# Q's second projection moved up behind kv, one mixer chunk moved ahead of the outputs, and x's blocks fetched in 4 loads

## The chip, the cores and the metric

The kernel runs on one NeuronCore of a Trainium2 chip. The metric is device time in microseconds of one execution. TensorE (PE in the profile; PEld is its weight loads), VectorE (DVE), ScalarE (ACT), GpSimd (POOL) and SyncE (SP, which issues the DMA loads and stores) run their own instruction streams in order and wait for each other on semaphores.

## The reference

Per batch (8 of them, 576 tokens) there is a linear attention over 8 heads with 128 exponential features, and then a token mixer of rank 32 and a two-layer network of width 2048:

```python
def phi(x):
    proj = np.einsum('bhsd,df->bhsf', x, w_phi)
    proj = proj - np.max(np.abs(proj), axis=-1, keepdims=True)
    return np.concatenate([np.exp(proj), np.exp(-proj)], axis=-1)
q_p, k_p = (phi(q), phi(k))
kv = np.einsum('bhsf,bhsd->bhfd', k_p, v)
z = np.sum(k_p, axis=2)
num = np.einsum('bhsf,bhfd->bhsd', q_p, kv)
den = np.einsum('bhsf,bhf->bhs', q_p, z)[..., None] + 1e-06
x = num / den                     # heads side by side: (8, 576, 512)
u = x + (x.transpose(0, 2, 1) @ U @ V).transpose(0, 2, 1)
out = u + np.maximum(u @ w_ch1, 0.0) @ w_ch2
```

## The kernel before

**Attention** goes by pairs of heads, four pairs to a batch, 32 in all. A pair (`Pair`, named b_j) has seven steps on TensorE: `s_project_k0` (products pkt, pk00, pk01), `s_out` of the pair before it (xpt, xp0, xp1), `s_project_k1` (pk10, pk11, pqt), `transposes` of the pair after it, `s_project_q0` (pq0), `s_kv` (kv_ps) and `s_project_q1` (pq1). Each q projection runs through a chain: ScalarE copies it (L394), GpSimd takes a maximum over partitions (L395), VectorE subtracts it (L396), ScalarE takes two exponentials (L397, L398); `s_out` needs the result, and it uses q1's (qp1) last, in xp1.

From batch 2 on (`SPLIT`), q and k come in as blocks (`raw`, 4 loads of 64 KB each for k and for q), which VectorE turns in place (L347) and splits into two parts, `T0` for k and `T1` for q (L350 on ScalarE, L351 on VectorE). `T1` has one buffer, so the next pair's T1 waits until pq1 has been computed, and the loads for the pair after that wait until T1 has been made from the block buffer. VectorE's L347 for a later pair stands ahead of L396 of qp1 in VectorE's order.

**The mixer** of batch g is cut into 32 chunks (`Mixer.chunks`): `hidden(f)` (product ph, 12 matrix products, then h_hi on ScalarE and h_lo on VectorE, L666) and `add(f)` (o, 12 products), f from 0 to 15, in the order h0, h1, a0, h2, a1, ... h15, a14, a15. ph has one PSUM bank, so a hidden chunk waits for the h_lo of the one before. `Pace.step()` puts the chunks of the batch before between the attention steps, 28 per batch; 4 are held back (`HELD`) until the batch's end.

**The end of a batch** is `tokens()`: the token mixing down (pp) and up (vp), x with the mixing added is stored to DRAM (`u_dram`, L618), and read back as blocks (`y`, L646, 16 loads), which VectorE turns (L652) and splits with ScalarE into uT_hi and uT_lo, from which the next mixer starts. The residual rows `st` are read from `u_dram` too (L690) and added at the end (L700). Attention products and vp share three PSUM banks (tag "at") in turn.

The order on TensorE is the written one from the tenth pair on; on the other engines, and on SyncE's queue, a scheduler places the instructions ahead of the run. Three chunks' worth of mixer weights are read again in each batch (`stream`, L218).

Of the kernel before, what the change touches and what calls it, by code (L numbers as in the profile page):

```python
# [21 lines left out]
P = 128  # L22
# [3 lines left out]
def tile_kernel(  # L26
# [12 lines left out]
    nc = tc.nc  # L39
    B, H, S, D = q.shape  # L40
# [91 lines left out]
    def scratch(name, dt=F32, shape=(2, 512)):  # L132
        return moe.tile([P, *shape], dt, tag="wide", bufs=NW, name=name)
# [132 lines left out]
    class Pair:  # L266
# [276 lines left out]
        def s_kv(self):  # L543
            self.kv_tail()
            self.kv_main(0, self.kp0)
            self.kv_main(1, self.kp1)
            self.kv_done()

        def s_out(self, x, xt):
            self.out_tail(xt)  # L550
# [70 lines left out]
    class Mixer:  # L621
        def __init__(self, g, x):
            self.g, self.x = g, x
            self.uT_hi = moe.tile([P, NCC, 512], F32R, tag="uT_hi", name=f"uT_hi{g}")
            self.uT_lo = moe.tile([P, NCC, 512], F32R, tag="uT_lo", name=f"uT_lo{g}")
            self.o, self.h = None, {}

        def transposes(self, t):
            pt = ps(f"pt{self.g}_{t}", "at" if 0 < self.g and t < 2 or self.g >= B - 1 else "o")
# [10 lines left out]

        def load_blocks(self):
            self.y = home.tile([P, NCC, SM], F32, tag="w_late", name=f"y{self.g}")
            for c in range(NCC):
                for i in range(4):
                    cs = slice(c * P + i * Q, c * P + (i + 1) * Q)
                    nc.sync.dma_start(  # L646
                        out=self.y[i * Q:(i + 1) * Q, c, :].rearrange("r (j e) -> r j e", e=Q),
                        in_=u_dram[self.g][:, cs].rearrange("(j r) e -> r j e", r=Q))

        def turn_blocks(self, c):  # L650
            y = self.y[:, c, :]
# [3 lines left out]
        def hidden(self, f):  # L655
            ph = ps(f"ph{self.g}_{f}", "at" if self.g >= B - 1 and f % 2 == 0 else "ph")
            n = 0
            for c in range(NCC):
                for l, r in ((0, self.uT_hi), (0, self.uT_lo), (1, self.uT_hi)):
                    mm(  # L660
                        ph, w1_part(f, l, c), r[:, c, :], start=(n == 0), stop=(n == 3 * NCC - 1))
                    n += 1
            h_hi = moe.tile([P, 512], F32R, tag="h_hi", bufs=2, name=f"h_hi{self.g}_{f}")
            h_lo = moe.tile([P, 512], F32R, tag="h_lo", bufs=2, name=f"h_lo{self.g}_{f}")
            on_act = nc.scalar.activation(out=h_hi, in_=ph, func=AF.Relu)  # L665
            on_dve = nc.vector.scalar_tensor_tensor(  # L666
                out=h_lo, in0=ph, scalar=0.0, in1=f32(h_hi), op0=ALU.max, op1=ALU.subtract)
            self.h[f] = (h_hi, h_lo)
            if self.g == 0:
                made.append((on_act, on_dve))  # L670
            if f in STREAM:
                stream(0, self.g, f)

        def add(self, f):
            if self.o is None:
                self.o = [ps(f"o{self.g}_{t}", "o") for t in range(4)]
            h_hi, h_lo = self.h.pop(f)
            for t in range(4):
                cs = slice(t * P, (t + 1) * P)
                for n, (l, r) in enumerate(((h_hi, 0), (h_hi, 1), (h_lo, 0))):  # L680
                    mm(
                        self.o[t], l[:, cs], w2_t[f][:, r, :],
                        start=(f == 0 and n == 0), stop=(f == NFC - 1 and n == 2))
            if f in STREAM:
                stream(1, self.g, f)
            if f == NFC - 3 and self.g < B:
                self.res = []
                for t in range(0, 4, 2):
                    st = scratch(f"st{self.g}_{t}")
                    nc.sync.dma_start(out=st, in_=u_rows(self.g)[:, t:t + 2, :])  # L690
                    self.res += [st[:, 0, :], st[:, 1, :]]
            if f == NFC - 1:
                self.finish()

        def finish(self):
            g = self.g
            for t in range(4):
                if g < B:
                    st = self.res[t]
# [101 lines left out]
    def tokens(tk, fill):  # L801
# [11 lines left out]
        other()  # L813
        pace.step()
        tk.down(1)
        other()
        pace.step()
        tk.up(0)
        tk.up(1)
        if tk.b >= SPLIT:  # L820
            tk.up(2)
            tk.up(3)
            m = Mixer(tk.b, tk.x)
            m.load_blocks()
            pace.step()
            other()
            pace.step()
            tk.up(NT)
            mix(len(todo) - HELD)
            for c in range(NCC):  # L830
                m.turn_blocks(c)
                mix(c % 2)
            todo.extend(m.chunks())
            return
# [36 lines left out]
    if True:  # L871
# [18 lines left out]
        for n, (b, j) in enumerate(pairs):  # L890
# [8 lines left out]
                    weights(LOADS[n])  # L899
            if nxt is not None:  # L900
                step(nxt.s_project_k0)
            step(cur.s_out, x, xt)
            if nxt is not None:
                step(nxt.s_project_k1)
# [4 lines left out]
            if j == NPAIR - 1:  # L909
                fill = []  # L910
                if nxt is not None:
                    fill = [far.transposes, nxt.s_project_q0, nxt.s_kv, nxt.s_project_q1]
                if b == 0:
                    pieces.extend(first_tokens(tk))
                    pieces.pop(0)()
# [11 lines left out]
            else:  # L927
# [7 lines left out]
                        pace.step()  # L935
                step(nxt.s_project_q0)
                step(nxt.s_kv)
                step(nxt.s_project_q1)
            cur, nxt = nxt, far
        mix(len(todo) - HELD)  # L940
        x = moe.tile([P, NT, C], F32, tag="x", name="x_tail")
# [39 lines left out]
```

## Time and profile before

| | |
|---|---|
| median of three executions | 1217.95 us (1217.53 to 1222.39) |
| the profiled execution's own time | 1218.95 us |
| its span, first to last instruction | 1217.2 us |
| TensorE busy | 1143.4 us (94%) |
| VectorE busy | 678.6 us (56%) |
| ScalarE busy | 536.9 us (44%) |
| GpSimd busy | 204.0 us (17%) |
| DMA bytes moved | 110.29 MB, mean 91 GB/s |

Read it as one long stream of matrix products with small gaps: the gaps, and stretches in which the granted clock is low, are all that can be won without taking products away. Batches 0 and 1 run until about 240 us, the paired stretches of batches 2 to 7 with a mixer beside them until about 1010 us, and the rest is mixer alone.

### The profile page before, as it was taken

The numbers are of one execution on the slowest core, as the hardware profiler recorded it, in microseconds if no ns is written. First come the engines' busy times: TensorE is split into PE (matmuls) and PEld (weight loads), VectorE is DVE, ScalarE is ACT, GpSimd is POOL, SyncE is SP. The second block draws the span as 40 slices with busy tenths as digits, with TensorE's granted clock in tenths as the row PEclk, the third lists the DMA queues.
The fourth block names the chain that finished last, engine by engine and source line by source line (L and its number), as shares of the span: only waits on it lengthen the run. The fifth ranks groups of instructions, "written<-read, shape, count | busy, mean of one in ns | idle before, by whom it ended". The sixth has DMA issues, their size and how long they took to land.

```text
span 1217.2 us, 22306 instructions
## 1 busy us (share of the span) xinstructions
PE 1143.4 (94%) x8845; PEld 940.3 (77%) x8845; DVE 678.6 (56%) x1482; ACT 536.9 (44%) x1151; POOL 204.0 (17%) x154
## 2 busy tenths in 40 slices
PE   8989988999998999899998999899999999999998
PEld 6767866778887887677787887687877878888886
DVE  5567798765556656754556566765656533312111
ACT  6678877454434544343434544344434431011110
POOL 4234453211110121011110121011201110000000
PEclk8999999999999999998999999999999999999999
DMA  5785421422353234422353233422342115410201
GB/s 144 224 264 199 134 57 20 138 65 65 82 117 94 52 63 112 102 49 63 82 118 93 55 64 106 106 66 55 92 102 80 36 53 160 121 52 15 75 15 35
DMA packets 247944, 110.29 MB, mean 91 GB/s; under 512 B 212640, under 2 KB 225184, under 8 KB 247840
## 3 DMA queue, kind: packets, MB, share of 16 engines
q1 hardware_dynamic: 247520, 108.34, 33.4%
q8 instruction: 70, 1.15, 0.4%
q10 hardware_dynamic: 320, 0.52, 0.1%
q14 instruction: 34, 0.28, 0.1%
HBM read 86.80 MB, written 22.02 MB: 89 GB/s over the span
## 4 chain that ended last, share of the span: by engine, by line
PE 65%; DVE 14%; SPq 6%; ACT 6%; DMA 5%; issue 2%; POOL 1%; DVEq 0%; POOLq 0%; ACTq 0%
PE o L79 24%; PE ph L79 23%; PE kv_ps L79 6%; PE xp L79 4%; SPq L291 3%; SPq L646 3%; DMA raw<-in_q_dram 3%; PE pq L79 2%; DVE T L351 2%; PE pk L79 2%; PE pp L79 1%; DVE uT_lo L259 1%; DVE h_lo L666 1%; DVE x L615 1%; DMA raw<-in_k_dram 1%
## 5 line engine op out<-in xcount | busy, mean ns | idle before, releaser
L79 PE MATMUL ph<-uT_hi,w 128*128 128x512 f32 x1152 | 387.9, 398 | 12.3 <-DVE h_lo L666 11.0
L79 PE MATMUL o<-w,h_hi 128*128 128x512 f32 x1152 | 358.8, 397 | 0.8 <-ACT h_hi L665 0.7
L79 PEld LDWEIGHTS ph<-uT_hi,w 128*128 128x128 f32 x1152 | 217.9, 189 | 63.3 <-DVE h_lo L666 14.7
L79 PEld LDWEIGHTS o<-w,h_hi 128*128 128x128 f32 x1152 | 213.9, 190 | 46.6 <-ACT h_hi L665 2.1
L79 PE MATMUL ph<-uT_lo,w 128*128 128x512 f32 x576 | 226.7, 394 | 2.4 <-DVE uT_lo L259 2.4
L79 PE MATMUL o<-w,h_lo 128*128 128x512 f32 x576 | 222.2, 394 | 0.3 <-DVE h_lo L666 0.3
L666 DVE SCALAR_TENSOR_TENSOR h_lo<-ph,h_hi 128x512 fp32r<-128x512 f32 x144 | 98.5, 684 | 220.0 <-ACT h_hi L665 219.7
L665 ACT ACTIVATE h_hi<-ph 128x512 fp32r<-128x512 f32 x144 | 85.7, 595 | 296.5 <-PE ph L79 296.2
L395 POOL PARTITION_ALL_REDUCE qp<-qp x64 | 128.8, 2012 | 339.5 <-ACT qp L394 339.2
L79 PEld LDWEIGHTS o<-w,h_lo 128*128 128x128 f32 x576 | 109.0, 190 | 24.2 <-DVE h_lo L666 0.8
L79 PEld LDWEIGHTS ph<-uT_lo,w 128*128 128x128 f32 x576 | 109.2, 190 | 23.6 <-DVE uT_lo L259 2.9
L79 PE MATMUL xp<-kv,qp 128*64 128x65 f32 x2048 | 87.5, 241 | 42.3 <-ACT qp L397 17.2
L79 PEld LDWEIGHTS xp<-kv,qp 128*64 128x64 f32 x2048 | 76.1, 153 | 55.3 <-ACT qp L397 21.9
L351 DVE TENSOR_TENSOR T<-raw,T 64x512 fp32r<-64x512 f32 x96 | 68.5, 714 | 34.7 <-ACT T L350 32.0
L395 POOL PARTITION_ALL_REDUCE qp_t<-qp_t x32 | 25.6, 800 | 358.9 <-ACT qp_t L394 358.9
L397 ACT ACTIVATE qp<-qp 128x512 f32<-128x512 f32 x64 | 40.2, 629 | 93.4 <-DVE qp L396 93.3
L350 ACT CAST T<-raw 64x512 fp32r<-64x512 f32 x96 | 59.4, 619 | 38.1 <-PE pq L79 36.8
L79 PE MATMUL kv_ps<-vb,kp 128*64 128x65 f32 x2048 | 70.0, 224 | 0.0
L79 PEld LDWEIGHTS kv_ps<-vb,kp 128*64 128x64 f32 x2048 | 63.8, 137 | 6.9 <-issue 2.0
L385 ACT ACTIVATE kp<-kp 128x512 f32<-128x512 f32 x64 | 40.3, 630 | 63.3 <-DVE kp L382 63.3
L347 DVE STREAM_TRANSPOSE raw<-raw 128x512 f32<-128x512 f32 x48 | 34.1, 711 | 47.2 <-DMA raw<-in_k_dram 27.7
L155 POOL INT64_ADD w_ab<-w_ab x32 | 43.6, 1363 | 71.7 <-DVE w_ab L151 59.8
(119 smaller groups left out, 1282.2 us busy)
## 6 DMA issues: line engine op xcount, KB each, us to landing
w<-kept SPq DMA_DIRECT2D x46, 512.0 KB, 3.8
words<-in_moe_w_ch_dram SPq DMA_DIRECT2D x32, 512.0 KB, 7.4
vb<-in_v_dram SPq DMA_DIRECT2D x64, 128.0 KB, 3.0
u_dram<-x SPq DMA_DIRECT2D x32, 256.0 KB, 2.1
st<-u_dram SPq DMA_DIRECT2D x16, 512.0 KB, 3.9
out_dram<-st SPq DMA_DIRECT2D x32, 256.0 KB, 2.1
y<-u_dram SPq DMA_DIRECT2D x112, 64.0 KB, 2.4
raw<-in_k_dram SPq DMA_DIRECT2D x96, 64.0 KB, 2.3
```

Of the source, the lines that this page charges most:

```text
L79: ins = nc.tensor.matmul(*args, **kw)
L155: nc.gpsimd.int64_add(a64, a64, b64)
L291: self.loaded = nc.sync.dma_start(out=to[i * Q:(i + 1) * Q], in_=src[b, self.h0 + i // 2, 0:SM, cs].rearrange("(j c) r -> c j r", c=Q))
L347: nc.vector.transpose(out=x_, in_=x_)
L350: nc.scalar.copy(out=m[here, s, :], in_=x_[here])
L351: nc.vector.tensor_sub(m[there, s, :], x_[here], f32(m[here, s, :]))
L385: nc.scalar.activation(out=kp[:, :, 0:F], in_=kp[:, :, F:2 * F], func=AF.Exp)
L395: nc.gpsimd.partition_all_reduce(qp[:, 0, :], qp[:, 1, :], P, ReduceOp.absmax)
L397: nc.scalar.activation(out=qp[:, 0, :], in_=qp[:, 1, :], func=AF.Exp)
L646: nc.sync.dma_start(out=self.y[i * Q:(i + 1) * Q, c, :].rearrange("r (j e) -> r j e", e=Q), in_=u_dram[self.g][:, cs].rearrange("(j r) e - ...
L665: on_act = nc.scalar.activation(out=h_hi, in_=ph, func=AF.Relu)
L666: on_dve = nc.vector.scalar_tensor_tensor(out=h_lo, in0=ph, scalar=0.0, in1=f32(h_hi), op0=ALU.max, op1=ALU.subtract)
```

## The change

Seven edits. (1) From batch 2 on, `s_project_q1` is issued inside `s_kv`, right behind the kv products, and the chunk that stood after it now stands as a second one between `s_project_k0` and the previous pair's `s_out`. (2) At the end of such a batch the fill list is one shorter, and the token products come in twos, with a chunk between. (3) `y` is fetched by 4 loads of 256 KB instead of 16 of 64 KB, each for 32 partitions and all four groups of columns. (4) The residual loads are issued after the second `down`, in a method of their own. (5) The streamed weights' loads are issued two chunks (`hidden`) or one (`add`) later in the code. (6) `tk.late` replaces an equal condition. (7) Line numbers behind the edits move by 2 to 10.

```diff
@@ -545,6 +545,8 @@
             self.kv_main(0, self.kp0)
             self.kv_main(1, self.kp1)
             self.kv_done()
+            if self.split:
+                self.s_project_q1()
 
         def s_out(self, x, xt):
             self.out_tail(xt)
@@ -623,7 +625,7 @@
             self.g, self.x = g, x
             self.uT_hi = moe.tile([P, NCC, 512], F32R, tag="uT_hi", name=f"uT_hi{g}")
             self.uT_lo = moe.tile([P, NCC, 512], F32R, tag="uT_lo", name=f"uT_lo{g}")
-            self.o, self.h = None, {}
+            self.o, self.h, self.res = None, {}, None
 
         def transposes(self, t):
             pt = ps(f"pt{self.g}_{t}", "at" if 0 < self.g and t < 2 or self.g >= B - 1 else "o")
@@ -640,12 +642,11 @@
 
         def load_blocks(self):
             self.y = home.tile([P, NCC, SM], F32, tag="w_late", name=f"y{self.g}")
-            for c in range(NCC):
-                for i in range(4):
-                    cs = slice(c * P + i * Q, c * P + (i + 1) * Q)
-                    nc.sync.dma_start(
-                        out=self.y[i * Q:(i + 1) * Q, c, :].rearrange("r (j e) -> r j e", e=Q),
-                        in_=u_dram[self.g][:, cs].rearrange("(j r) e -> r j e", r=Q))
+            of = u_dram[self.g].rearrange("(j r) (c i e) -> i r c j e", r=Q, i=4, e=Q)
+            for i in range(4):
+                nc.sync.dma_start(
+                    out=self.y[i * Q:(i + 1) * Q].rearrange("r c (j e) -> r c j e", e=Q),
+                    in_=of[i])
 
         def turn_blocks(self, c):
             y = self.y[:, c, :]
@@ -668,8 +669,8 @@
             self.h[f] = (h_hi, h_lo)
             if self.g == 0:
                 made.append((on_act, on_dve))
-            if f in STREAM:
-                stream(0, self.g, f)
+            if f - 2 in STREAM:
+                stream(0, self.g, f - 2)
 
         def add(self, f):
             if self.o is None:
@@ -681,19 +682,22 @@
                     mm(
                         self.o[t], l[:, cs], w2_t[f][:, r, :],
                         start=(f == 0 and n == 0), stop=(f == NFC - 1 and n == 2))
-            if f in STREAM:
-                stream(1, self.g, f)
-            if f == NFC - 3 and self.g < B:
-                self.res = []
-                for t in range(0, 4, 2):
-                    st = scratch(f"st{self.g}_{t}")
-                    nc.sync.dma_start(out=st, in_=u_rows(self.g)[:, t:t + 2, :])
-                    self.res += [st[:, 0, :], st[:, 1, :]]
+            if f - 1 in STREAM:
+                stream(1, self.g, f - 1)
             if f == NFC - 1:
                 self.finish()
 
+        def residual(self):
+            self.res = []
+            for t in range(0, 4, 2):
+                st = scratch(f"st{self.g}_{t}")
+                nc.sync.dma_start(out=st, in_=u_rows(self.g)[:, t:t + 2, :])
+                self.res += [st[:, 0, :], st[:, 1, :]]
+
         def finish(self):
             g = self.g
+            if g < B and not self.res:
+                self.residual()
             for t in range(4):
                 if g < B:
                     st = self.res[t]
@@ -813,17 +817,18 @@
         other()
         pace.step()
         tk.down(1)
+        if todo:
+            todo[0][0].__self__.residual()
         other()
         pace.step()
         tk.up(0)
         tk.up(1)
-        if tk.b >= SPLIT:
+        if tk.late:
+            pace.step()
             tk.up(2)
             tk.up(3)
             m = Mixer(tk.b, tk.x)
             m.load_blocks()
-            pace.step()
-            other()
             pace.step()
             tk.up(NT)
             mix(len(todo) - HELD)
@@ -899,6 +904,8 @@
                     weights(LOADS[n])
             if nxt is not None:
                 step(nxt.s_project_k0)
+                if nxt.split:
+                    pace.step()
             step(cur.s_out, x, xt)
             if nxt is not None:
                 step(nxt.s_project_k1)
@@ -909,7 +916,9 @@
             if j == NPAIR - 1:
                 fill = []
                 if nxt is not None:
-                    fill = [far.transposes, nxt.s_project_q0, nxt.s_kv, nxt.s_project_q1]
+                    fill = [far.transposes, nxt.s_project_q0, nxt.s_kv]
+                    if not nxt.split:
+                        fill.append(nxt.s_project_q1)
                 if b == 0:
                     pieces.extend(first_tokens(tk))
                     pieces.pop(0)()
@@ -935,7 +944,8 @@
                         pace.step()
                 step(nxt.s_project_q0)
                 step(nxt.s_kv)
-                step(nxt.s_project_q1)
+                if not nxt.split:
+                    step(nxt.s_project_q1)
             cur, nxt = nxt, far
         mix(len(todo) - HELD)
         x = moe.tile([P, NT, C], F32, tag="x", name="x_tail")
```

On TensorE, in the middle of a batch (pair 4_1, mixer of batch 3; of each chunk only its first row is left, "..." stands for the rest of it). Before:

```order
L79 MATMUL kv_ps4_1_5825<-vb1_97,kp4_1_1_5718 64x65 x16
L79 MATMUL ph3_2_5862<-uT_hi3_5451,w1_2_1336 128x512
...
L79 MATMUL pq1_4_1_5879<-T1_4_1_5341,w_hl_88 128x512 x2
L79 MATMUL o3_0_5807<-w2_1_1265,h_hi3_1_5794 128x512 x2
...
L79 MATMUL pk01_4_2_5931<-w_hl_88,T0_4_2_5765 128x256 x2
L79 MATMUL ph3_3_5941<-uT_hi3_5451,w1_3_1443 128x512
...
L79 MATMUL xpt4_1_5958<-kv4_1_5860,qp4_1_t_5737 64x65 x4
L79 MATMUL xp0_4_1_5971<-kv4_1_5860,qp4_1_0_5801 64x65 x16
L79 MATMUL xp1_4_1_5992<-kv4_1_5860,qp4_1_1_5882 64x65 x16
```

and of the change:

```order
L79 MATMUL kv_ps4_1_5816<-vb1_97,kp4_1_1_5711 64x65 x16
L79 MATMUL pq1_4_1_5853<-T1_4_1_5341,w_hl_88 128x512 x2
L79 MATMUL o3_0_5772<-w2_1_1265,h_hi3_1_5749 128x512 x2
...
L79 MATMUL pk01_4_2_5907<-w_hl_88,T0_4_2_5756 128x256 x2
L79 MATMUL ph3_3_5917<-uT_hi3_5481,w1_3_1443 128x512
...
L79 MATMUL o3_0_5772<-w2_2_1400,h_hi3_2_5810 128x512 x2
...
L79 MATMUL xpt4_1_5946<-kv4_1_5851,qp4_1_t_5730 64x65 x4
L79 MATMUL xp0_4_1_5959<-kv4_1_5851,qp4_1_0_5791 64x65 x16
L79 MATMUL xp1_4_1_5980<-kv4_1_5851,qp4_1_1_5856 64x65 x16
```

Between pq1 and xp1 there were two chunks, and there are three.

On VectorE, at the end of batch 3 (vp is the token product whose result is added to x, raw4_3 a block load of a later pair, y3 the blocks read back, h_lo2 the old mixer's), from the last two x adds on. Before:

```order
L615 TENSOR_TENSOR x3_4207<-x3_4207,vp3_3_5447 128x512
L351 TENSOR_TENSOR T1_4_1_5341<-raw4_1_5148,T1_4_1_5341 64x512 x2
L615 TENSOR_TENSOR xt2_2826<-xt2_2826,vp3_4_5508 64x512
L666 SCALAR_TENSOR_TENSOR h_lo2_13_5505<-ph2_13_5491,h_hi2_13_5504 128x512
L652 STREAM_TRANSPOSE y3_5453<-y3_5453 128x512
L396 TENSOR_TENSOR qp4_0_1_5485<-qp4_0_1_5485 128x512
L652 STREAM_TRANSPOSE y3_5453<-y3_5453 128x512 x2
L666 SCALAR_TENSOR_TENSOR h_lo2_14_5538<-ph2_14_5524,h_hi2_14_5537 128x512
L652 STREAM_TRANSPOSE y3_5453<-y3_5453 128x512
L924 MEMSET xt4_5586 64x512
L347 STREAM_TRANSPOSE raw4_3_5900<-raw4_3_5900 128x512
```

and of the change:

```order
L347 STREAM_TRANSPOSE raw4_3_5876<-raw4_3_5876 128x512
L396 TENSOR_TENSOR qp4_0_1_5430<-qp4_0_1_5430 128x512
L617 TENSOR_TENSOR x3_4195<-x3_4195,vp3_2_5473 128x512
L617 TENSOR_TENSOR x3_4195<-x3_4195,vp3_3_5477 128x512
L667 SCALAR_TENSOR_TENSOR h_lo2_13_5470<-ph2_13_5456,h_hi2_13_5469 128x512
L347 STREAM_TRANSPOSE raw4_3_5876<-raw4_3_5876 128x512
L617 TENSOR_TENSOR xt2_2826<-xt2_2826,vp3_4_5500 64x512
L667 SCALAR_TENSOR_TENSOR h_lo2_14_5518<-ph2_14_5504,h_hi2_14_5517 128x512
L653 STREAM_TRANSPOSE y3_5483<-y3_5483 128x512 x4
L380 TENSOR_REDUCE mk4_1_t_5586<-pkt4_1_5582 128x1
L933 MEMSET xt4_5562 64x512
L667 SCALAR_TENSOR_TENSOR h_lo2_15_5559<-ph2_15_5545,h_hi2_15_5558 128x512
```

The turn of raw4_3 now stands ahead of the last x adds and of h_lo2_13, and all four turns of y3 stand ahead of h_lo2_15, which stood behind the uT_lo splits before.

On SyncE's queue at the same place. Before:

```order
L320 DMA vb0_91<-in_v_dram 128x4x64 x2
L618 DMA u_dram3_110<-x3_4207 128x512 x4
L646 DMA y3_5453<-u_dram3_110 32x16x32 x16
L618 DMA u_dram8_115<-xt2_2826 64x512
L291 DMA raw4_3_5900<-in_k_dram 32x16x32 x4
L291 DMA raw4_3_5900<-in_q_dram 32x16x32 x4
```

and of the change:

```order
L320 DMA vb0_91<-in_v_dram 128x4x64 x2
L291 DMA raw4_3_5876<-in_k_dram 32x16x32 x4
L620 DMA u_dram3_110<-x3_4195 128x512 x2
L291 DMA raw4_3_5876<-in_q_dram 32x16x32 x4
L620 DMA u_dram3_110<-x3_4195 128x512 x2
L647 DMA y3_5483<-u_dram3_110 32x64x32 x4
L620 DMA u_dram8_115<-xt2_2826 64x512
```

The block loads of raw4_3 moved from behind the loads of y to before them, between the stores that y waits for.

## Rows read from the trace of the kernel before

**Rows 1.** The page, engines: busy us, share of the span, instructions.

```profile
PE 1143.4 (94%) x8845; PEld 940.3 (77%) x8845; DVE 678.6 (56%) x1482; ACT 536.9 (44%) x1151; POOL 204.0 (17%) x154
```

**Rows 2.** TensorE's waits, 240 to 1040 us: waiter, releaser, total us, times, longest.

```profile
PE xp L79 <- DVE kp L435: 13.4, 5, 3.2
PE xp L79 <- ACT qp L397: 11.4, 11, 2.3
PE xp L79 <- ACT qp L398: 10.4, 18, 0.8
PE ph L79 <- DVE h_lo L666: 8.8, 6, 1.6
```

**Rows 3.** Two batches by stretch: length, busy us by engine, granted clock, DMA.

```profile
504.19:644.29 140.10, 130.19 (x1038) 107.74 (x1038) 81.14 (x182) 59.52 (x132) 18.88 (x12) 0.95 0.33 80
644.29:777.85 133.56, 125.25 (x1037) 104.42 (x1038) 81.95 (x183) 59.52 (x132) 19.16 (x12) 0.99 0.35 84
```

**Rows 4.** Timeline of TensorE, one pair: start, us, operation, [idle before <-releaser].

```profile
559.16 0.62 PE L79 MATMUL pq<-T,w_hl 128*128 128x512 f32 x2
...
568.95 0.34 PE L79 MATMUL xp<-kv,qp 128*64 128x65 f32 x4 [1.69 <-ACT qp L397]
570.07 1.79 PE L79 MATMUL xp<-kv,qp 128*64 128x65 f32 x28 [0.79 <-ACT qp L398]
```

**Rows 5.** Timeline of VectorE, the same pair.

```profile
560.47 1.40 DVE L351 TENSOR_TENSOR T<-raw,T 64x512 fp32r<-64x512 f32 x2 [3.62 <-ACT T L350]
...
566.95 0.71 DVE L347 STREAM_TRANSPOSE raw<-raw 128x512 f32<-128x512 f32 x1 [1.65 <-DMA raw<-in_k_dram]
567.58 0.65 DVE L396 TENSOR_TENSOR qp<-qp 128x512 f32<-128x512 f32 x1
```

**Rows 6.** Timeline of TensorE at the last pair of all.

```profile
993.88 0.34 PE L79 MATMUL xp<-kv,qp 128*64 128x65 f32 x4 [2.29 <-ACT qp L397]
```

**Rows 7.** Stretches of low granted clock: length, busy us of PE, PEld, DVE, ...; clock.

```profile
269.10:272.50 3.40, 3.07 (x35) 2.62 (x34) 1.99 (x9) 0.64 (x2) 0.00 (x0) 0.51 0.02 5
538.80:542.20 3.40, 3.40 (x9) 2.61 (x9) 2.43 (x8) 1.63 (x5) 0.00 (x0) 0.50 0.00 0
569.50:576.30 6.80, 6.23 (x39) 5.14 (x40) 2.64 (x12) 1.04 (x2) 0.00 (x0) 0.50 0.00 1
```

**Rows 8.** Timeline of TensorE at the end of batch 3.

```profile
475.57 0.50 PE L79 MATMUL ph<-uT_hi,w 128*128 128x512 f32 x1
...
483.12 0.39 PE L79 MATMUL ph<-uT_hi,w 128*128 128x512 f32 x1
...
485.84 0.39 PE L79 MATMUL vp<-pst,v_all 128*128 128x512 f32 x1
...
504.19 3.36 PE L79 MATMUL xp<-kv,qp 128*64 128x65 f32 x64 [3.25 <-DVE kp L435]
...
515.92 0.50 PE L79 MATMUL ph<-uT_hi,w 128*128 128x512 f32 x1 [1.60 <-DVE h_lo L666]
```

**Rows 9.** Timeline of VectorE at the same place.

```profile
481.25 0.68 DVE L615 TENSOR_TENSOR x<-x,vp 128x512 f32<-128x512 f32 x1
...
494.38 0.71 DVE L652 STREAM_TRANSPOSE y<-y 128x512 f32<-128x512 f32 x1 [0.79 <-DMA y<-u_dram]
...
500.11 0.71 DVE L347 STREAM_TRANSPOSE raw<-raw 128x512 f32<-128x512 f32 x1 [1.06 <-DMA raw<-in_q_dram]
500.75 2.45 DVE L259 TENSOR_TENSOR uT_lo<-y,uT_hi 128x512 fp32r<-128x512 f32 x4
...
508.75 2.73 DVE L700 TENSOR_TENSOR st<-st,o 128x512 f32<-128x512 f32 x4 [0.33 <-PE o L79]
```

**Rows 10.** Timeline of SyncE's DMA issues at the same place.

```profile
479.57 2.71 SPq L618 DMA_DIRECT2D u_dram<-x  x4
484.10 8.29 SPq L646 DMA_DIRECT2D y<-u_dram  x16
```

**Rows 11.** DMA, 484 to 494.5 us: packets, MB, share of 16 engines; loads, KB, landing us.

```profile
q1 hardware_dynamic: 8748, 1.21, 70.6%
...
y<-u_dram SPq DMA_DIRECT2D x16, 64.0 KB, 2.3
```

## The prediction

> **What bounds the kernel now.** The page's engine row comes first: TensorE is busy for 94% of the span, the next engine for 77% only as TensorE's own weight loads, VectorE for 56% [rows 1]. No product is removed, so only TensorE's gaps and its slow stretches can be won. The view of waits then says who opens the gaps between 240 and 1040 us, where attention and mixer are interleaved [rows 2]. Two kinds stand out. xp waits for ScalarE's two exponentials of qp (L397, L398): 11.4 and 10.4 us, up to 2.3 us at a time. And once per batch end xp waits for VectorE's kp (L435), 13.4 us in 5 waits, followed by a wait of ph for h_lo, 8.8 us in 6. Third, the stretches: one batch takes 140.10 us where the next takes 133.56, with a granted clock of 0.95 against 0.99 [rows 3]. The low stretches stand at half clock (1.2 of 2.4 GHz) and begin within two us of a wait for qp [rows 4, 7]. So the gaps cost twice.
>
> **The middle of a batch.** Moving pq1 ahead of a chunk and a chunk behind `s_project_k0` adds one chunk between pq1 and xp1. A chunk is 485.84 - 483.12 = 2.72 us [rows 8]. What is late is a chain that hangs on pq1: T1 can be overwritten after it, T1's split ends at 560.47 + 1.40 = 561.87, the block loads go out, VectorE stands still until 566.95 for the turn of raw, and only then does the subtraction of qp1 (567.58) follow [rows 5]. From pq1's start at 559.16 the turn is 7.8 us away, and it takes xp1 to 568.95 and 570.07 to have both halves [rows 4]. The whole chain starts one chunk earlier relative to xp1, so a wait of up to 2.72 us goes to nothing. The worst here is 1.69 + 0.79 = 2.48 us [rows 4]. Only the last pair of all has no next pair, hence no second chunk: its 2.29 us stay [rows 6]. Gain: 11.4 + 10.4 - 2.3 = **19.5 us**.
>
> The pair's other waits: kv_ps must leave its bank before pk00, three products later in that tag, with one chunk less between. The copy of kv is the next thing on VectorE and a chunk is 2.72 us; I cost it at nothing, with one VectorE step (0.7 us [rows 9]) per pair if that cover fails, 16 us over 23 pairs, as the upper bound.
>
> **The slow clock in the middle.** The three low stretches away from the batch ends follow such waits, and TensorE is busy in them for 3.07, 3.40 and 6.23 us [rows 7]; at full clock half of that is saved, **6.3 us** (bounds 0 and 6.3). That agrees with rows 3, where 140.10 - 133.56 = 6.5 us is the two later stretches' 4.8 plus longer waits. I take all of it, since the waits ahead go.
>
> **The end of a batch.** Here the change does three things: pq1 goes up, add(15) runs before xp (it fills the wait for kp: 2.72 us for a mean of 13.4 / 5 = 2.7), and VectorE's and SyncE's orders are new. The second is worth nothing if VectorE is late with something else. So I follow VectorE, counted from kv's end, 475.57 [rows 8]. Today the second hidden chunk starts at 515.92, 40.35 us later; one chunk now stands before kv, so 37.6 us are to be beaten. In the new order: pq1 at 0; raw4_3's turn, in front of the x adds, can start 7.8 us after pq1, as in the middle of a batch [rows 4, 5]; the turn 0.71, qp1's subtraction 0.65, two x adds 0.68 each: 10.5. From the end of the last x add to y's first load is 484.10 - 481.93 = 2.2 us [rows 9, 10]: 12.7. Then y lands, and **how long four big loads take is not in the trace**.
>
> Lower bound: 8748 packets took 70.6% of 16 engines for 10.5 us, 13.6 ns each [rows 11]. y is 1 MB in pieces of 128 bytes, 8192 packets, so 6.9 us with all engines full, and 1.9 us of fixed time (a 64 KB load lands 2.3 us after its issue, of which 0.4 are its packets): 8.8 us. Upper bound: as today, from 484.10 until the last turn starts at 494.38, 10.3 us [rows 9, 10]. I take 9.3, nearer the lower one, since 16 issues of 0.5 us [rows 10] no longer set the pace: 22.0. All four turns stand behind the last load now, 4 x 0.71: 24.9. Behind them is a string of VectorE work that is the same as today's from uT_lo to the last st, 508.75 + 2.73 - 500.75 = 10.7 us [rows 9], plus kp_t and the next mixer's h_lo, 1.3 us (an estimate from the 0.7 us steps): 36.9 us, against 37.6. So at the batch ends one wait takes the place of another: **0.6 us** in each of five, **3 us**. On the way h_lo13 stands behind raw4_3's turn, and TensorE waits about 1 us for it; it is inside the 36.9. Bounds: all of both waits, 13.4 + 5 x 1.6 = 21.4 us, if raw and y come early; below, y's lateness one for one, 5 us per us.
>
> The Trainium skill, "DMA: Bandwidth & Descriptors", Rules for kernel authors, says to coalesce small transfers, since under 64 KB one pays mostly overhead; its table of loads measured on another queue has 6.15 us for 1 MB, and by that, an estimate, the batch ends would give 5 x 3.1 = 16 us more, 1173. The trace disagrees as far as packets go: 8192 of 13.6 ns are there in either form [rows 11], so my sum stays with the bounds above.
>
> **Edits costed at nothing.** The residual loads are issued before finish() by a whole batch end as now, and a late one costs its 3 to 4 us of landing only if nothing stands between. The streamed weights have two chunks or more (5.4 us) until use. In the first two batches nothing moves until pair 1_3; around batch 1's end the scheduler's order changes in both directions, 0 with bounds of 3 us either way. The last mixer alone keeps its products.
>
> **Sum.** 19.5 + 6.3 + 3 = 28.8 us off the profiled execution's own 1218.95: 1190. The median of the runs stands 1.0 us below that execution, so **1189 us**.
>
> **Rivals.**
> *The batch end opens too* (0.19). If raw4_3 and y land early, VectorE keeps up, and kp's and h_lo's waits go as well: 21.4 in place of 3: 1171. For it speaks that SyncE issues raw4_3 before y, and that today's wait at 504.19 ends behind a turn of raw at 500.11 that waited for its load [rows 8, 9]. Against it, the turns of y can no longer run between loads.
> *The wait for qp shrinks by half only* (0.20). If raw's loads hang on the v loads ahead of them in SyncE's queue, which wait for kv and don't move, the chain moves less than a chunk. Half of 19.5 and half of 6.3 stay: 1202. Against it: the turn starts 5.1 us after T1's split ends [rows 5], so T1 releases it today.
> *The other side: y's loads run at half rate* (0.07). Each load writes only 32 partitions; if it ran on half of the engines, y would take 13.9 + 1.9 = 15.8 us instead of 9.3, 6.5 us later at five ends, 32 us: 1222, and 5 us more for each us beyond. It decides when y takes 9.3 + 28.8 / 5 = 15.1 us. For it: in the old form neighbouring loads on different partitions overlapped. Against it: today's loads also write 32 partitions each and fill 70.6% of 16 engines [rows 11]. The Trainium skill, same page, section "Why a DMA increments its semaphore by 16 and not by 1", has the number of engines set by the slowest dimension on both sides; that is 32 in both forms, so by that rule this rival fails, and the 70.6% agrees.
> *Gains given back in small new waits* (0.08), PSUM banks above all, the 16 us above together with a late y: within 0.5%, about 1214.
>
> **Numbers.** The forecast has 0.46. 0.5% (6 us) is about what a measurement here can tell from no change. Faster by more: 0.46 + 0.19 + 0.20 = 0.85; within: 0.08; slower by more: 0.07. The range runs from 1166 (the second case with less raw time) to 1208 (the third with one us of y's lateness); it leaves out the last two cases and the edge of the second. The likeliest case's own range is 1180 to 1198.
>
> **What would show it.** In the waits, xp behind L397 and L398 falls from 21.8 us to about 3, the rest at the last pair. The batch of 140 us takes what its neighbours take, and the clock at mid-batch stays up. At the batch ends kp's wait is gone, and TensorE waits instead for h_lo13, h_lo15 or a bank that VectorE frees late, some 4 us in all; y's turns start 9 us after its first load. I am wrong if raw's turn or y lands more than two us off, or if pk00 begins to wait for kv.

## The result, and the profile after

The changed kernel takes 1190.46 us (median of 4 runs, 1189.84 to 1192.87) against 1219.61 us of the kernel before (4 runs, 1217.53 to 1222.39): the ratio is 0.976, interval 0.974 to 0.979. The forecast was 1189 us. The profiled execution took 1189.84 us, its span is 1188.1 us.

The page's engine row, which answers to [rows 1], has 12.5 us less of busy TensorE, though the products are the same (a few of their records are missing from the trace):

```profile
PE 1130.9 (95%) x8841; PEld 932.3 (78%) x8845; DVE 671.6 (57%) x1482; ACT 538.9 (45%) x1151; POOL 202.5 (17%) x154
```

TensorE's waits between 240 and 1040 us, as in [rows 2] (waiter, releaser, total us, times, longest):

```profile
PE o L79 <- DVE h_lo L667: 15.3, 6, 3.5
PE ph L79 <- DVE h_lo L667: 7.7, 8, 2.6
PE xp L79 <- ACT qp L397: 2.3, 1, 2.3
PE ph L79 <- DVE uT_lo L259: 1.1, 1, 1.1
PE pk L79 <- DVE xt L493: 0.7, 1, 0.7
...
PE xp L79 <- ACT qp L398: 0.3, 1, 0.3
```

The waits for qp fell from 21.8 to 2.6 us, and these stand at the last pair. The wait of xp for kp is gone. In its place o, the products of a batch's last `add`, waits for h_lo15: 15.3 us in 6, five of them at the batch ends.

The middle of a batch, the pair that answers to [rows 4, 5]: first TensorE, then VectorE (start, us, operation, [idle before <-releaser]).

```profile
544.92 0.73 PE L79 MATMUL pq<-T,w_hl 128*128 128x512 f32 x2
...
554.77 2.04 PE L79 MATMUL xp<-kv,qp 128*64 128x65 f32 x64
```

```profile
546.34 1.40 DVE L351 TENSOR_TENSOR T<-raw,T 64x512 fp32r<-64x512 f32 x2 [0.87 <-ACT T L350]
...
552.65 0.71 DVE L347 STREAM_TRANSPOSE raw<-raw 128x512 f32<-128x512 f32 x1 [1.45 <-DMA raw<-in_k_dram]
553.28 0.65 DVE L396 TENSOR_TENSOR qp<-qp 128x512 f32<-128x512 f32 x1
```

The turn of raw still starts 7.7 us after pq1 and still waits for its load, but xp starts 9.85 us after pq1 and runs through in one row of 64.

Batch end 3, which answers to [rows 8 to 10]: TensorE, VectorE, SyncE's issues.

```profile
466.54 0.73 PE L79 MATMUL pq<-T,w_hl 128*128 128x512 f32 x2
...
477.90 0.50 PE L79 MATMUL ph<-uT_hi,w 128*128 128x512 f32 x1 [1.31 <-DVE h_lo L667]
...
493.75 0.80 PE L79 MATMUL o<-w,h_lo 128*128 128x512 f32 x1 [3.50 <-DVE h_lo L667]
...
505.55 0.50 PE L79 MATMUL ph<-uT_hi,w 128*128 128x512 f32 x1 [0.76 <-DVE h_lo L667]
```

```profile
474.76 0.71 DVE L347 STREAM_TRANSPOSE raw<-raw 128x512 f32<-128x512 f32 x1 [2.56 <-DMA raw<-in_k_dram]
...
489.66 2.49 DVE L653 STREAM_TRANSPOSE y<-y 128x512 f32<-128x512 f32 x4 [7.38 <-DMA y<-u_dram]
...
493.00 0.69 DVE L667 SCALAR_TENSOR_TENSOR h_lo<-ph,h_hi 128x512 fp32r<-128x512 f32 x1
```

```profile
473.88 2.26 SPq L291 DMA_DIRECT2D raw<-in_q_dram  x4
476.67 0.94 SPq L620 DMA_DIRECT2D u_dram<-x  x2
479.46 6.62 SPq L647 DMA_DIRECT2D y<-u_dram  x4
```

Read them together: VectorE stands still for 7.38 us until y lands, turns all four blocks in one go, and only then comes to h_lo15, whose input had long been there. TensorE stands for 3.50 us. The same wait at the other four ends is 2.78, 2.54, 3.49 and 2.63 us. The Trainium skill, "PSUM — Partial Sum Buffer", Engine vs sequencer instructions, has VectorE's queue strictly first in, first out, and these rows agree: 7.38 us of idle VectorE with h_lo15 behind the turns.

The windows that answer to [rows 3] and [rows 7] (stretch, length, busy us of PE, PEld, DVE, ACT, POOL, granted clock, DMA share, GB/s):

```profile
498.81:626.43 127.62, 124.03 (x1042) 103.88 (x1042) 79.75 (x181) 59.95 (x132) 18.80 (x12) 0.98 0.38 86
626.43:755.05 128.62, 124.36 (x1043) 104.02 (x1041) 81.02 (x185) 60.12 (x132) 18.63 (x12) 0.98 0.40 88
492.60:499.40 6.80, 5.65 (x30) 4.26 (x32) 6.77 (x14) 0.82 (x3) 0.00 (x0) 0.51 0.10 39
622.30:625.70 3.40, 3.40 (x9) 2.67 (x9) 3.40 (x8) 0.62 (x2) 0.00 (x0) 0.52 0.00 0
```

The batch of 140.10 us and its neighbour of 133.56 us [rows 3] now take 127.6 and 128.6. The three stretches of half clock (1.2 of 2.4 GHz) away from the batch ends [rows 7] are gone. Those at the batch ends are not: there are four, two of them 6.8 us long now, and each begins next to the wait for h_lo15. Two of 3.4 us are new, at the last pair's wait for qp (from 960.3 us) and at 997.9 us. So between 240 and 1040 us half clock fell only from 30.7 to 27.3 us in all, which is worth 1.7 us of time.

### The profile page after: what moved, and what is told of

Read it like the earlier page. It is cut to its first block, busy times and chain, and to the rows that moved or that the text cites. A ratio compares the mean times of both kernels' runs of the same rounds, so it can differ in the third digit from the quotient of the medians.

```text
span 1188.1 us, 22127 instructions
## 1 busy us (share of the span) xinstructions
PE 1130.9 (95%) x8841; PEld 932.3 (78%) x8845; DVE 671.6 (57%) x1482; ACT 538.9 (45%) x1151; POOL 202.5 (17%) x154
## 4 chain that ended last, share of the span: by engine, by line
PE 69%; DVE 13%; DMA 8%; SPq 4%; ACT 4%; issue 2%; POOL 1%; DVEq 0%; ACTq 0%; POOLq 0%
PE ph L79 26%; PE o L79 25%; PE kv_ps L79 5%; PE xp L79 4%; DMA y<-u_dram 3%; PE pq L79 2%; DMA raw<-in_k_dram 2%; PE pk L79 2%; SPq L647 2%; DVE T L351 1%; PE pp L79 1%; DMA u_dram<-x 1%; SPq L291 1%; DVE w L250 1%; DVE y L653 1%
## 5 line engine op out<-in xcount | busy, mean ns | idle before, releaser
L79 PEld LDWEIGHTS o<-w,h_hi 128*128 128x128 f32 x1152 | 216.5, 191 | 46.4 <-ACT h_hi L666 1.9
L79 PE MATMUL o<-w,h_lo 128*128 128x512 f32 x576 | 226.4, 401 | 15.3 <-DVE h_lo L667 15.3
L395 POOL PARTITION_ALL_REDUCE qp<-qp x64 | 127.6, 1994 | 261.4 <-ACT qp L394 229.9
L79 PE MATMUL xp<-kv,qp 128*64 128x65 f32 x2048 | 72.3, 225 | 9.9 <-ACT qp L397 7.7
L79 PEld LDWEIGHTS xp<-kv,qp 128*64 128x64 f32 x2048 | 66.0, 140 | 17.3 <-ACT qp L397 9.6
L396 DVE TENSOR_TENSOR qp<-qp 128x512 f32<-128x512 f32 x64 | 46.4, 725 | 14.7 <-POOL qp L395 14.5
```

What stands on the lines that cost most here:

```text
L79: ins = nc.tensor.matmul(*args, **kw)
L395: nc.gpsimd.partition_all_reduce(qp[:, 0, :], qp[:, 1, :], P, ReduceOp.absmax)
L396: nc.vector.tensor_sub(qp[:, 1, :], qp[:, 1, :], qp[:, 0, :])
```

## The experiments

Eleven kernels. Ratios are to the kernel before, timed on the same chip in the same rounds (its medians there were 1222.45, 1223.32 and 1219.85 us); the changed kernel's is 0.976.

**Where the second chunk stands.** First it goes back behind `s_out`:

```diff
             step(nxt.s_project_k0)
-            if nxt.split:
-                pace.step()
         step(cur.s_out, x, xt)
+        if nxt is not None and nxt.split:
+            pace.step()
```

> The changed kernel with the second mixer chunk put back behind the attention outputs; Q's second projection still follows kv. From pq1 to xp1 there are then two chunks again, as in the kernel before. Theory (the chunk between pq1 and xp1 is what pays): the waits of xp for qp come back to 15 to 22 us in all, the slow-clock stretches in mid-batch come back, one or more, and xp waits for kp again at the five batch ends: 1210 to 1220 us. Rival (the new place of pq1 next to kv is what pays, wherever the chunk stands): xp's waits for qp stay under 5 us and the time is 1190 to 1197 us.

1221.6 us, ratio 1.000 (0.998 to 1.002). Its waits, same stretch:

```profile
PE xpt L79 <- DVE kp L435: 17.9, 5, 4.5
PE xp L79 <- ACT qp L398: 10.8, 18, 0.8
PE xp L79 <- ACT qp L397: 8.7, 11, 2.3
```

The qp waits are back at 19.5 us and kp's at 17.9: without this chunk the whole gain is gone, and the time is just above the expected range. One thing the theory expected did not come: between 240 and 1000 us no stretch of half clock lies away from a batch end. But the longest waits did not come back either. In the kernel before, the stretches that begin at 269.1 and 538.8 us stand at these rows of xp (the third stands at [rows 4]):

```profile
268.93 0.34 PE L79 MATMUL xp<-kv,qp 128*64 128x65 f32 x4 [1.98 <-ACT qp L397]
...
534.38 1.10 PE L79 MATMUL xp<-kv,qp 128*64 128x65 f32 x32
536.95 0.34 PE L79 MATMUL xp<-kv,qp 128*64 128x65 f32 x4 [1.47 <-ACT qp L397]
537.62 1.04 PE L79 MATMUL xp<-kv,qp 128*64 128x65 f32 x28 [0.33 <-ACT qp L398]
```

In each, TensorE waits twice for qp within one row of 64 products, 2.3, 1.8 and 2.5 us in all; these are the three longest there before the last pair, the next is 1.4. With the chunk behind, the longest is 1.75 us:

```profile
268.94 0.34 PE L79 MATMUL xp<-kv,qp 128*64 128x65 f32 x4 [1.05 <-ACT qp L397]
269.98 1.04 PE L79 MATMUL xp<-kv,qp 128*64 128x65 f32 x28 [0.70 <-ACT qp L398]
```

So this run speaks neither for nor against long waits as the reason of those stretches. The same kernel with sixteen loads of y (next part) was the fourth corner:

> The changed kernel with sixteen loads of y again and the second mixer chunk behind the attention outputs: the fourth corner beside the changed kernel (ratio to before 0.976), the one with sixteen loads (0.962) and the one with the chunk behind (1.000). Theory (the chunk ahead of the outputs pays the same with either form of y's loads, 2.3 % of the time before): ratio 0.985, 1204 us, xp's waits for qp back at about 19 us. Rival (with y early enough the batch end no longer needs the chunk): the chunk is worth little more than the qp waits, 19.5 us less the last pair's 2.3: ratio 0.976, 1193 us.

1207.24 us, ratio 0.987 (0.985 to 0.989). The chunk is worth 2.3 to 2.5% with either form of the loads: the two edits add up. One stretch of half clock (302.8 us) is off the batch ends here, behind a row of xp with 1.64 us of waits. The third place for the chunk separates kp's distance from qp's:

```diff
         if nxt is not None:
+            if nxt.split:
+                pace.step()
             step(nxt.s_project_k0)
-            if nxt.split:
-                pace.step()
         step(cur.s_out, x, xt)
```

> The changed kernel with sixteen loads of y, and with the second mixer chunk ahead of K's first projection instead of behind it: from pq1 to xp1 there are three chunks as in the changed kernel, from K's first projection to the outputs only one, as in the kernel before. So the prediction's first term (the qp waits) stands alone, without its last (a chunk that fills the wait for kp at the batch ends). Theory (two separate waits): xp's waits for qp stay at 2 to 4 us, the wait for kp at the five batch ends stays at 13 to 18 us; with the chunk behind the outputs the ratio was 0.987, ahead of them 0.962; 17 us of the 31 between them for the qp waits leave ratio 0.973, 1190 us. Rival (the qp waits are all of it): 0.962 to 0.965. Rival (the batch ends are most of it): 0.980 or more.

1176.01 us, ratio 0.965 (0.963 to 0.967), at the edge of the first rival's range. The waits for qp are 2.6 us, as expected; but kp's fell as well, to 0.8 us, with only one chunk between K's projection and the outputs, as in the kernel before. So the theory of two separate waits fell. At batch end 3 VectorE makes kp (L435) only behind all four turns of y and h_lo15, and a chunk ahead of the outputs gives it time, on either side of K's projection.

**How y is loaded.** The four loads alone, in the kernel before:

```diff
-            for c in range(NCC):
-                for i in range(4):
-                    cs = slice(c * P + i * Q, c * P + (i + 1) * Q)
...
+            for i in range(4):
+                nc.sync.dma_start(
+                    out=self.y[i * Q:(i + 1) * Q].rearrange("r c (j e) -> r c j e", e=Q),
+                    in_=of[i])
```

> The kernel before with the four 256 KB loads of y alone. Theory (the coalescing is worth nothing, and takes from VectorE the turns between the loads): the last load of y lands within 1 us of the kernel before, the turns follow it as one group of 2.5 us, and each of five batch ends gets 0 to 2 us longer: 1219.6 to 1230 us. Rival (fewer, larger loads land sooner, as the prediction had it, 9.3 us in place of 10.3): 1214 to 1219 us. Rival (each large load uses few DMA engines): over 1235 us.

1241.33 us, ratio 1.015 (1.014 to 1.017): this edit by itself makes the kernel 19 us slower. At batch end 3, TensorE and VectorE:

```profile
504.31 0.79 PE L79 MATMUL ph<-uT_hi,w 128*128 128x512 f32 x1 [4.29 <-DVE h_lo L665]
```

```profile
500.39 2.49 DVE L651 STREAM_TRANSPOSE y<-y 128x512 f32<-128x512 f32 x4 [6.48 <-DMA y<-u_dram]
...
503.56 0.69 DVE L665 SCALAR_TENSOR_TENSOR h_lo<-ph,h_hi 128x512 fp32r<-128x512 f32 x1
```

The loads were issued from 489.66 on, so the first turn starts 10.7 us later; and waits of ph for h_lo went from 8.8 us [rows 2] to 30.3 in ten. The time lies in the second rival's range, but its reason is out: y takes as long as in the kernel before, 10.3 us [rows 9, 10]. The theory had only the turns in it and not what is queued behind them, nor the half clock, which rose from 30.7 to 50.9 us between 240 and 1040 us. The other way round, the changed kernel with the sixteen loads back:

> The changed kernel with y's sixteen 64 KB loads back in place of the four of 256 KB; all else as changed. Theory (four loads land no sooner than sixteen, 10.2 us against 10.3 us, and now all four turns of y stand behind the last load): y lands as before, but three of its four turns run while the last loads are still under way, so VectorE's string behind y is about 2 us shorter at each of five batch ends: 1190.5 - 10 = 1181 us, and the four waits of o for h_lo15 (2.5 to 3.5 us each) shrink by about 2 us each. Rival A (four loads spare SyncE's queue): y's last load lands 1 to 3 us later than with four, the time is 1192 to 1200 us. Rival B (the place of y's turns sets nothing at the batch ends): 1190 to 1191 us.

1176.32 us, ratio 0.962 (0.960 to 0.964), 18 us faster than the changed kernel (0.0146 x 1222), where 10 were expected. VectorE at the same batch end, and the windows of two batches:

```profile
481.08 0.71 DVE L654 STREAM_TRANSPOSE y<-y 128x512 f32<-128x512 f32 x1 [1.43 <-DMA y<-u_dram]
484.18 0.71 DVE L654 STREAM_TRANSPOSE y<-y 128x512 f32<-128x512 f32 x1 [2.39 <-DMA y<-u_dram]
486.62 0.71 DVE L654 STREAM_TRANSPOSE y<-y 128x512 f32<-128x512 f32 x1 [1.73 <-DMA y<-u_dram]
...
488.95 0.70 DVE L654 STREAM_TRANSPOSE y<-y 128x512 f32<-128x512 f32 x1
489.58 0.65 DVE L668 SCALAR_TENSOR_TENSOR h_lo<-ph,h_hi 128x512 fp32r<-128x512 f32 x1
```

```profile
492.80:617.90 125.10, 122.69 (x1038) 102.53 (x1037) 80.48 (x184) 60.04 (x132) 18.65 (x12) 1.00 0.38 89
617.90:742.41 124.51, 122.08 (x1038) 102.47 (x1037) 80.76 (x181) 59.67 (x132) 18.89 (x12) 1.00 0.38 90
```

The first load is issued at 476.99. The last turn starts 12 us later, no sooner than with four loads (10.2 us), but it waits for VectorE's uT_lo and not for its load, and it is the only one left by then. The 8 us beyond the expectation go with the clock: in these batches it is 1.00, not 0.98. Between 240 and 1040 us the stretches of half clock add up to 3.4 us here and 27.3 in the changed kernel; half of the difference is 12 us at most, and the waits are 6.8 us less in all. The spans differ by 15.9. All executions bear the clock out: 0.988 to 0.991 in the five here, 0.981 to 0.986 in the four of the changed kernel.

Is it the size of the loads or the place of the turns? The first attempt reversed the sixteen loads:

```diff
-            for c in range(NCC):
+            for c in reversed(range(NCC)):
                 for i in range(4):
```

> The changed kernel with sixteen loads of y, issued from the last column block to the first, while VectorE still turns the first block first: all four turns stand behind y's last load, as with four loads, but the loads are small. Theory (the four loads cost 17 us because no turn can run before the last one lands): ratio 0.974 to 0.978, 1189 to 1194 us, with clock dips at the batch ends. Rival (small loads are better by themselves, on the queue or in the DMA engines, or leave other loads alone): ratio 0.962, 1174 to 1178 us.

1175.29 us, ratio 0.961 (0.959 to 0.964). That looks like the rival, but its first turn starts 4.1 us after the first load, as with the loads in order: the turns are independent, and the scheduler reversed them too. So the run does not decide between the two. With each turn held behind the one before it, and h_lo15 behind the last:

```diff
+            with ExitStack() as order:
+                if c:
+                    order.enter_context(tc.issue_after(self.turned.ins))
+                self.turned = nc.vector.transpose(out=y, in_=y)
-            nc.vector.transpose(out=y, in_=y)
...
+                with tc.issue_after(m.turned.ins):
+                    mix(c % 2)
-                mix(c % 2)
```

> The changed kernel with sixteen loads of y again, issued from the last column block to the first, and with VectorE's four turns held to the order first to last, h_lo15 behind them: no turn can start before y's last load, exactly as with four loads, but the loads are the small ones. (In the run before this one, with the loads reversed alone, the turns were reversed with them, so that it tested nothing.) Theory (four loads cost 17 us because no turn can run before the last load lands): ratio 0.973 to 0.979, 1190 to 1197 us, o's waits for h_lo15 back at 12 us or more in five, clock dips at the batch ends. Rival (small loads are better by themselves): ratio 0.960 to 0.965.

1189.2 us, ratio 0.976 (0.974 to 0.978), that of the changed kernel. Its waits and VectorE at batch end 3:

```profile
PE o L79 <- DVE h_lo L671: 15.0, 6, 3.3
```

```profile
491.75 2.49 DVE L657 STREAM_TRANSPOSE y<-y 128x512 f32<-128x512 f32 x4 [2.32 <-DMA y<-u_dram]
494.17 0.65 DVE L671 SCALAR_TENSOR_TENSOR h_lo<-ph,h_hi 128x512 fp32r<-128x512 f32 x1
```

Small loads with the turns behind the last one cost the same as large loads: TensorE's waits between 240 and 1040 us are 28.1 us in both kernels. Here y's first load is issued at 480.84, and the first turn starts 10.9 us later, against 10.2 with four loads. So what the four loads cost is the place of the turns, and what it brings behind it, not the transfer.

**h_lo15 first.** If VectorE's order is the trouble, it can be mended with the four loads:

```diff
             mix(len(todo) - HELD)
+            mix(2)
             for c in range(NCC):
-                m.turn_blocks(c)
-                mix(c % 2)
+                with tc.issue_after(last[0].ins):
+                    m.turn_blocks(c)
```

(`last[0]` is the instruction that writes the newest h_lo.)

> The changed kernel with the turns of y behind h_lo15 in VectorE's order (h_lo15 is no longer held by turns that wait for y). Theory (VectorE's whole string behind y sets the end of the batch, so h_lo15's own 0.65 us comes off it and no more): the waits of o for h_lo15 (14.9 us in 5) go, but TensorE stands about as long behind uT_lo or the next mixer's h_lo: 1184 to 1189 us. Rival (o's wait for h_lo15 is what the batch end costs): 14.9 us less, 1174 to 1178 us. Either way the new wait for h_lo14 near 998 us goes as well if y7's turns follow it, 2.6 us of that.

1182.91 us, ratio 0.968 (0.966 to 0.970): 10 us faster than the changed kernel, between the two. Waits:

```profile
PE pk L79 <- DVE xt L493: 12.2, 5, 2.9
PE ph L79 <- DVE h_lo L667: 4.6, 4, 2.6
PE o L79 <- DVE h_lo L667: 2.4, 2, 1.3
```

The wait of o fell to 2.4 us, and the next pair's pk now waits 12.2 us for its PSUM bank, which VectorE frees at the end of the same string: the string behind y still sets the end. The wait of 2.64 us at 998 us is gone. With sixteen loads:

> The changed kernel with sixteen loads of y and with y's turns behind h_lo15 in VectorE's order. Theory (with sixteen loads three turns fit between h_lo15 and the last landing, so h_lo15 can go first for nothing): the waits of o for h_lo15 (8.7 us in 6 with sixteen loads alone) fall to under 2 us and no other wait takes their place: ratio 0.955, 1167 to 1170 us. Rival (the wait moves to the next product that VectorE feeds, pk for xt's bank, 12.2 us in 5 where h_lo15 went first with four loads): ratio 0.960 to 0.965, 1173 to 1179 us.

1170.24 us, ratio 0.957 (0.954 to 0.960). The waits of o are gone, and 6.4 us for xt's bank remain: halfway between the two expectations, nearer the theory.

**The remaining edits, and the last pair.**

```diff
-            if f - 2 in STREAM:
-                stream(0, self.g, f - 2)
+            if f in STREAM:
+                stream(0, self.g, f)
...
-        if todo:
-            todo[0][0].__self__.residual()
```

(likewise in `add`, with the residual loads back at f == NFC - 3.)

> The changed kernel with sixteen loads of y, and with the residual loads and the streamed weights issued where the kernel before issues them. Theory (these two edits change nothing on the path): ratio 0.960 to 0.964, 1173 to 1179 us. Rival (they keep transfers out of the way of y or raw, or a streamed weight comes late): ratio 0.966 or more, over 1181 us, with waits of ph or o for a w that a load fills.

1176.23 us, ratio 0.961 (0.959 to 0.964): no change, as expected. Last, on top of the kernel with h_lo15 first and sixteen loads, a chunk ahead of the last pair's outputs, in place of the one behind them:

```diff
             if nxt is not None:
                 step(nxt.s_project_k0)
                 if nxt.split:
                     pace.step()
+            else:
+                pace.step()
             step(cur.s_out, x, xt)
...
-            if nxt is None or not nxt.split:
+            if nxt is not None and not nxt.split:
                 pace.step()
```

> Sixteen loads of y and h_lo15 ahead of y's turns, as in the fastest run so far (ratio 0.957), and for the last pair, which has no next one, a mixer chunk ahead of its outputs. Theory: the last waits for qp (2.29 and 0.33 us) go, and the clock dip behind them with 1.7 us: 3 to 4 us off, ratio 0.953 to 0.955. Rival (the chunk is only missing later, and the wait moves behind the outputs): ratio 0.957, no change.

1163.12 us, ratio 0.954 (0.952 to 0.956), the lowest of all, though the interval overlaps with that of the kernel without this chunk (0.954 to 0.960). The last waits for qp are gone from its trace. These are all its waits between 240 and 1040 us, 11.1 us against 28.1 of the changed kernel:

```profile
PE pk L79 <- DVE xt L493: 6.8, 5, 2.1
PE ph L79 <- DVE h_lo L668: 2.3, 3, 1.2
PE ph L79 <- DVE uT_lo L259: 2.0, 2, 1.1
```

## Why the prediction was right, and where it was not

**The time** was right to 1.5 us, in part by luck. Both profiled executions, compared by TensorE's kv rows: 29.1 us in all, of which 0.65 up to 254 us, 28.8 in the steps within batches (forecast 25.8), 2.3 in the five steps across batch ends (forecast 3), and 2.6 lost at the end (forecast 0). By cause it is another sum than the forecast's. Between 240 and 1040 us TensorE's waits fell from 47.9 to 28.1 us, so by 19.8. Half clock gave 1.7 us, where 6.3 were forecast. The rest is xp's own time, for which the forecast had no term: at full clock a row of 64 cut by waits takes 1.10 + 0.34 + 1.04 = 2.48 us of busy time (534.38 above), one that runs through takes 2.04 (554.77). Seventeen rows more were cut before, which makes some 7 us, an estimate. This missing term stood in for the half clock that the sum counted as gone and that came back elsewhere.

**The waits for qp**: 21.8 to 2.6, against 21.8 to 2.3. The mechanism is shown by moving the chunk away (19.5 us back) and to another place ahead of the outputs (2.6 us). The chain behind pq1 is as long as before; only the chunk covers it. So the rival by which the wait shrinks by half only is out.

**The slow clock in the middle**: the three stretches went, as forecast, but so did all waits in mid-batch, and no run parts the two. They stood at the three longest waits for qp. Yet the last pair's wait, 2.6 us and the same in both kernels, has a stretch in the changed kernel and none in the kernel before, and with the chunk behind the outputs 1.64 us had one and 1.75 us had none. So the length of the wait is not all of it, and the rest stays open. One profile is also one sample: in seventeen executions of the kernel before the mean granted clock ran from 0.977 to 0.985, which is some 20 us of half clock more or less (0.008 x 1220 x 2, an estimate).

**The batch ends**: the sum, 3 us, came out near 2.3, from steps that were off. Counted from kv's end in batch 3: raw's turn 8.2 us after pq1 (forecast 7.8); y's first load at 12.9 (12.7); the first turn 10.2 us behind it (9.3; the upper bound was 10.3); the last turn over at 25.6 (24.9); the second hidden chunk at 39.0 (36.9, with 37.6 to beat). That end lost 1.4 us where 0.6 were to be won, others won 0.4 to 1.6. Two terms were too small: y's **9.3 us**, and the string behind the turns, 36.9 - 24.9 = 12.0 us, which took 13.4 with the half clock that the sum had not priced. The prediction named h_lo15 among the new waits. Its "some 4 us in all" holds for one batch end and not for all five: its own sum leaves 13.4 + 5 x 1.6 - 3 = 18.4 us of waits there, and 20.7 were measured, 14.9 of them o's for h_lo15.

**The four loads** were priced as a gain of 1 us per end, since 16 issues no longer set the pace. They cost 18 to 19 us, and the rest of the change is worth some 46. What failed is the comparison: four turns behind the last load were added to the string, but the sixteen loads were never followed through the new order, in which only one turn is left behind the last. The coalescing rule (the Trainium skill, "DMA: Bandwidth & Descriptors", Rules for kernel authors) speaks of transfers under 64 KB, and these had 64; merged, y lands at about the same time, and what the pieces gave was the work between them. The 6.15 us that its table has for 1 MB is not reached here: y takes 10.2. The rival of half rate is out (10.2 us, not 15.8). The rival by which the batch end opens too had the right picture of what these ends could give; that its 1171 is the time with sixteen loads and h_lo15 first is chance, as its sum lacks xp's term too.

**Edits costed at nothing**: the stream and residual loads are shown to be nothing; pk00 never waits for kv. At the end it was wrong: the four turns of y7 hold h_lo14 too, and TensorE waits 2.64 us at 997.82, with 3.40 us of half clock beside it, and as much stands at the last pair's wait. Open remains what makes the kernel with sixteen loads and the chunk behind the outputs 16 us faster than the one before; the place of raw's loads at the batch ends and the stretches of half clock (13.6 against 30.7 us) both differ, and neither was tried alone.

## What to carry to other kernels

When a chain hangs on one product, move that product ahead of work that needs nothing from the chain. Here one chunk of 2.72 us paid nearly the whole wait, and it did so on either side of K's projection. A row of small products that waits no longer cut gets shorter by itself; count that too. Before you merge small loads, look at what runs between their landings: one load that everything waits for also holds back whatever stands behind its consumer in a queue that runs in order. Price a new place in such a queue by what is queued behind it, and add the half clock that may follow the new wait: a stretch that goes in one place can come back in another.

## What the hardware did that was not expected

Four loads of 256 KB landed at about the same time as sixteen of 64 KB: from the first issue to the turn that waits for the last load it is 10.2 us (changed kernel) and 10.7 (the four loads alone) against 10.3 [rows 9, 10] and 10.9 (sixteen loads, turns held). The DMA view of the changed kernel from 479.4 to 490 us, and of the kernel with sixteen loads from 476.9 to 489 us (queue: packets, MB, share of 16 engines; loads, KB each, median us to landing):

```profile
q1 hardware_dynamic: 8336, 1.18, 92.2%
...
y<-u_dram SPq DMA_DIRECT2D x4, 256.0 KB, 6.1
```

```profile
q1 hardware_dynamic: 8528, 1.18, 60.9%
...
y<-u_dram SPq DMA_DIRECT2D x16, 64.0 KB, 2.7
```

The packets are nearly the same in number, but each takes 0.922 x 16 x 10.6 / 8336 = 18.8 ns of an engine against 0.609 x 16 x 12.1 / 8528 = 13.8 ns; the prediction had 13.6 for either form. Four issues occupied SyncE for 6.62 us, sixteen for 9.31 us, so the issues are not free either: 1.7 us each in place of 0.6. So 6.6 of the 10.2 us pass before the last large load has been issued. Why packets slow down and issues are long when fewer, larger loads are under way was not tried.

The half clock follows small differences: in the changed kernel the waits of o at the batch ends (2.5 to 3.5 us) had such a stretch beside four of the five, and with sixteen loads of y (1.1 to 2.7 us) beside none. Three more kernels with sixteen loads (the loads reversed, the streams as before, the chunk ahead of K's projection) had waits of 0.8 to 2.6 us there and a stretch beside one or two.
